# A two-layer SSM and SwiGLU kernel: five small layer-norm products move from ScalarE to VectorE, and a new order of work takes the place of the old

## The chip, the cores and the metric

The kernel runs on one core of a Trainium2 chip. A core has five engines that work through their own queues: TensorE (matrix products; PE in the profile, its weight loads PEld), VectorE (DVE), ScalarE (ACT), GpSimd (POOL) and SyncE (SP, which here only issues DMA transfers). The metric is the device time of one execution in microseconds. The kernel before took 341.52 us, the median of three runs (341.47 to 341.84).

## What is computed

Four layers follow one another on a sequence of 2048 tokens with 512 features in bfloat16, two of kind A and two of kind B, each added to its input after a layer norm without weights:

```
x = A_q
x = x + A(layernorm(x))      # A(q): kv = shift_conv(k) * v;  y = long_conv(kv, ssm_k) + kv * ssm_D;  return q * y
x = x + B(layernorm(x))      # B(x): (silu(x @ w_gate) * (x @ w_up)) @ w_down,  512 -> 1792 -> 512
x = x + A(layernorm(x))
x = x + B(layernorm(x))
layernorm(x) = (x - mean(x)) / sqrt(var(x) + 1e-5)
```

The convolution y depends on k, v and ssm_k alone, so it is made once and both A layers use it.

## The kernel before

**Tiling.** The sequence is cut into four blocks c = 0 to 3 of 512 tokens, and a block into two halves h of 256 tokens (two rows of 128 tokens by 512 features in a tile `xc`). A unit of work is (layer, c, h). For each unit there are, in this order: the layer norm of A (`apply_norm`, L958), the product with the convolution `Yk` and the sum into `xc`, the layer norm of B (both in `prologue`, L967), a transpose of its result `z` to `zT` by DMA, and the feed-forward part `ffn` (L1124). There TensorE writes gate and up products to four PSUM buffers `pf`, ScalarE empties them (`sg` by Silu and `hr` or `ht` by a copy, L1111, L1112, L1171, L1175), VectorE multiplies the two (L1115, L1118, L1178), and TensorE multiplies by `w_down` into `pd` (L1198). Some groups turn `hr` back by a DMA transpose (L1120) into `sg`. The convolution (`conv`, L1441) goes through spectra: small Fourier products on TensorE, then long products and sums on VectorE (`product`, L719: `t<-X,G` at L744, `t<-t,t` and `Z<-t,t` at L748).

**A layer norm.** Each half needs mean and variance of its two rows. `ln_stats` (L895) takes them on VectorE, into a tile `mv`. `ln_stats_act` (L906) takes them on ScalarE with two passes over each row (`jk`), and ends with `nm` (minus the mean) and `ve` (variance plus eps). Either way `power` (L888, L891) then has GpSimd raise the 128x2 values to the power -0.5: this is the tile `rstd`. There are 32 such power steps in a run, 12 from `ve` and 20 from `mv`. The rows are then normalised (`normalise`, L944) by VectorE, which reads `rstd` (L952), or by ScalarE, which reads `rstd` and a shift `nmr`, minus the mean times `rstd` (L947). `shift_of` (L932) makes `nmr`: for statistics of VectorE as one operation of VectorE (L936), for statistics of ScalarE as two operations of ScalarE, one for each row (L940). The second kind occurs in five units: the norms of A in (0,0,0), (0,0,1), (0,3,0), (1,0,0) and (1,1,1), so L940 runs ten times.

**The order.** Every operation is entered by `add` with an engine, a cost and what it reads and writes. A list `ORDER` of 1721 numbers, written out in the file, gives each operation its place in one sequence, and each engine works through its own operations in that sequence. Nothing is sorted at run time: an engine whose next operation is not ready waits, with all that is queued behind it. `walk` (L230) goes through the sequence when the kernel is built, with the entered costs. What it works out is used for two things: which buffer of a ring each tile gets, and where the 33 filler products at the start stand (`issue`, L299). It does not change the order.

**GpSimd in the walk.** A VectorE operation that touches neither PSUM nor the norm's small statistics tiles is marked `two` (L187). `walk` lets a power step (`o.late` 1 from `mv`, 4 from `ve`) wait for one such VectorE operation that is under way when it begins, then ends it (`settle`, L237).

**In numbers of the sequence.** The power step of unit (1,0,0) stands at place 362, right behind its `ve` at 353. The two `nmr` on ScalarE stand at 368 and 371, with ScalarE's emptying of `pf` before, between and behind them (366, 367, 374, 382).

Of the kernel before, what the change touches and what calls it, by code (L numbers as in the profile page):

```python
# [32 lines left out]
TINY = 0.2  # L33
# [116 lines left out]
class Plan:  # L150
# [79 lines left out]
    def walk(self, seq, loads):  # L230
# [12 lines left out]
        for o in seq:  # L243
            if pend is not None and (o.eng == "POOL" or pend in o.preds):
                settle(0.0)
                pend = None
# [83 lines left out]
def kernel(  # L330
# [14 lines left out]
    nc = tc.nc  # L345
# [1171 lines left out]
```

## Time and profile before

| what | value |
|---|---|
| median of three runs | 341.52 us |
| the profiled execution, its own time | 341.52 us |
| its span, first to last instruction | 339.7 us |
| around the span | 1.8 us |
| TensorE busy | 333.5 us, 98% |
| VectorE busy | 299.7 us, 88% |
| ScalarE busy | 264.2 us, 78% |
| GpSimd busy | 35.5 us, 10% |
| granted TensorE clock | 1.00 |
| power steps from `ve` | 12, shortest 688, median 927, longest 5031 ns |
| power steps from `mv` | 20, shortest 685, median 770, longest 1031 ns |
| `nmr` on ScalarE (L940) | 10, median 294 ns |
| `nmr` on VectorE (L936) | 7, median 154 ns |

Lines of the profile name a place in the code (L891), an engine, an operation, the tile written and, behind an arrow, the tiles read. "x10" is a count. In a list of waits, the first name is the instruction that waited and the second what it waited for, and then come the total in us, the number of waits and the longest. In a timeline, the first number is the start and the second the length, and a bracket tells how long the engine had been idle and what released it.

### The profile page before, as it was taken

The page shows a single profiled execution, that of the slowest core. Times are in us where ns is not written, and L with a number is a line of the kernel's source. Part 1 is how long each engine was busy: PE and PEld are TensorE (multiplying, and loading weights), DVE is VectorE, ACT ScalarE, POOL GpSimd, SP SyncE. Part 2 cuts the span into 40 slices and gives each one's busy share as a digit, 9 for nine tenths or more (in the row PEclk, how much of TensorE's full clock was granted, in tenths as well). Part 3 has the DMA queues.
Part 4 walks back from the last instruction along what each step waited for, and adds up shares of the span by engine and source line. Part 5 has one row for each costly group of instructions (what it writes and reads, how often), then busy time and mean ns, then how long its engine had stood idle before and what let it go on. Part 6 is the DMA issues. An engine that isn't in the chain of part 4 may idle for free.

```text
span 339.7 us, 5935 instructions
## 1 busy us (share of the span) xinstructions
PE 333.5 (98%) x2172; PEld 204.9 (60%) x2172; DVE 299.7 (88%) x507; ACT 264.2 (78%) x544; POOL 35.5 (10%) x48
## 2 busy tenths in 40 slices
PE   9999999799999999999999999999999999999996
PEld 7766864544545564745445464654546587858884
DVE  7899999799788999999999999999998887966465
ACT  7999999698996675979899985989675547465373
POOL 4000112303010100102110100002001000100000
PEclk9999999999999999999999999999999999999999
DMA  7999602251417445382324244420504430123011
GB/s 271 339 294 367 122 8 56 51 127 39 94 31 96 93 108 125 62 147 59 62 43 83 46 92 127 93 48 3 105 17 94 65 78 11 39 48 77 2 34 62
DMA packets 77992, 31.59 MB, mean 93 GB/s; under 512 B 69765, under 2 KB 75786, under 8 KB 77962
## 3 DMA queue, kind: packets, MB, share of 16 engines
q1 hardware_dynamic: 77808, 31.13, 39.5%
q8 instruction: 17, 0.28, 0.3%
q14 instruction: 13, 0.11, 0.1%
q10 hardware_dynamic: 154, 0.07, 0.1%
HBM read 12.33 MB, written 2.10 MB: 42 GB/s over the span
## 4 chain that ended last, share of the span: by engine, by line
PE 89%; DVE 5%; ACT 3%; POOL 1%; DMA 1%; issue 1%
PE pf L402 54%; PE pd L1198 20%; PE ps L1073 7%; PE ps L402 6%; POOL rstd L891 1%; DVE t L734 1%; PE wm L1483 1%; DVE Z L738 1%; DMA sg<-hr 1%; DVE m L875 1%; PE pt L569 0%; DVE bst L900 0%; ACT jk L924 0%; DVE G L537 0%; ACT sg L1111 0%
## 5 line engine op out<-in xcount | busy, mean ns | idle before, releaser
L402 PEld LDWEIGHTS <-zT 128*128 128x128 bf16 x528 | 51.5, 98 | 60.6 <-DMA zT<-z 1.0
L402 PE MATMUL pf<-wu_sb,zT 128*128 128x512 bf16 x264 | 65.3, 379 | 0.0
L402 PE MATMUL pf<-wg_sb,zT 128*128 128x512 bf16 x264 | 65.2, 379 | 0.0
L1198 PE MATMUL pd<-wd_sb,sg 128*128 128x512 bf16 x200 | 49.3, 379 | 0.1
L402 PE MATMUL pf<-zT,wu_sb 128*128 128x256 bf16 x368 | 46.1, 272 | 1.8 <-ACT sg L1111 1.6
L1111 ACT ACTIVATE sg<-pf 128x512 bf16<-128x512 f32 x66 | 39.2, 611 | 10.0 <-PE pf L402 8.3
L402 PE MATMUL pf<-zT,wg_sb 128*128 128x256 bf16 x368 | 46.1, 273 | 0.0
L1112 ACT CAST hr<-pf 128x512 bf16<-128x512 f32 x66 | 38.1, 598 | 8.6 <-PE pf L402 7.8
L402 PEld LDWEIGHTS <-wu_sb 128*128 128x128 bf16 x368 | 36.0, 98 | 9.8 <-issue 2.6
L744 DVE TENSOR_TENSOR t<-X,G 128x4096 bf16<-128x4096 bf16 x18 | 41.1, 2285 | 0.0
L402 PEld LDWEIGHTS <-wg_sb 128*128 128x128 bf16 x368 | 36.0, 98 | 7.3
L1175 ACT CAST ht<-pf 128x512 bf16<-128x512 f32 x46 | 26.8, 598 | 12.1 <-PE pf L402 10.1
L1198 PEld LDWEIGHTS <-sg 128*128 128x128 bf16 x200 | 19.4, 98 | 22.3 <-DMA sg<-hr 1.0
L891 POOL TENSOR_TENSOR rstd<-mv,nhalf 128x2 f32<-128x2 f32 x20 | 16.7, 835 | 150.5 <-DVE mv L901 139.5
L1171 ACT ACTIVATE sg<-pf 128x512 bf16<-128x512 f32 x46 | 27.1, 614 | 6.5 <-PE pf L402 5.7
L1198 PE MATMUL pd<-wd_sb,ht 128*128 128x512 bf16 (+1 forms) x126 | 29.9, 369 | 0.0
L891 POOL TENSOR_TENSOR rstd<-ve,nhalf 128x2 f32<-128x2 f32 x12 | 15.2, 1268 | 121.5 <-ACT ve L928 121.5
L900 DVE BATCH_NORM_STATS2 bst<-xc 128x6 f32<-128x512 bf16 x40 | 26.5, 683 | 0.6
L1178 DVE TENSOR_TENSOR ht<-ht,sg 128x512 bf16<-128x512 bf16 (+1 forms) x31 | 16.6, 546 | 9.4 <-ACT ht L1175 7.5
L1118 DVE TENSOR_TENSOR hr<-hr,sg 128x1024 bf16<-128x1024 bf16 x27 | 18.5, 685 | 5.3 <-ACT sg L1111 3.0
L511 ACT ACTIVATE X<-ps 128x512 bf16<-128x512 f32 x32 | 19.1, 614 | 1.5 <-PE ps L402 0.9
L1198 PEld LDWEIGHTS <-ht 128*128 128x128 bf16 x126 | 12.3, 98 | 12.2 <-ACT z L947 0.2
(143 smaller groups left out, 528.3 us busy)
## 6 DMA issues: line engine op xcount, KB each, us to landing
hn<-in_A_ssm_k_dram SPq DMA_DIRECT2D x4, 512.0 KB, 6.0
vt<-in_A_v_dram SPq DMA_DIRECT2D x4, 512.0 KB, 8.8
xc<-in_A_q_dram SPq DMA_DIRECT2D x4, 512.0 KB, 5.4
out_dram<-xc SPq DMA_DIRECT2D x15, 128.0 KB, 1.8
wg_sb<-in_B_w_gate_dram SPq DMA_DIRECT2D x1, 1792.0 KB
wu_sb<-in_B_w_up_dram SPq DMA_DIRECT2D x1, 1792.0 KB, 7.9
wd_sb<-in_B_w_down_dram SPq DMA_DIRECT2D x1, 1280.0 KB
sg<-hr SPq DMA_TRANSPOSE x66, 2.4
```

Source lines behind the costliest of these rows:

```text
L402: nc.tensor.matmul(o, lhsT=lhsT, rhs=rhs, start=(n == 0), stop=(n == len(terms) - 1))
L511: add("ACT", act(D), lambda: nc.scalar.activation(out=view(), in_=ps.t[:], func=ACT.Copy, scale=scale), r=[ps], w=[(buf, keys)], conv=conv)
L744: dve(8 * D, lambda t=t, part=part: nc.vector.tensor_mul(out=t.t[:], in0=x.t[:, :, part:part + 1, :].to_broadcast((P, R, 2, D)), in1=g.t[: ...
L891: add("POOL", cost, lambda: nc.gpsimd.tensor_tensor(out=rstd.t[:], in0=var(), in1=nhalf.t[:].to_broadcast((P, n)), op=ALU.pow), r=reads + ...
L900: add("DVE", 0.6, lambda st=st, i=i: nc.vector.bn_stats(out=st.t[:, 0:6], in_=xs[c].t[:, i, :]), r=[(xs[c], (i,))], w=[st])
L1073: nc.tensor.matmul(bank.t[:, half_ * C:(half_ + 1) * C], lhsT=lhsT(i), rhs=rhs(i), start=(first and i == 0 and half_ == 0), stop=(last and ...
L1111: add("ACT", act(D), lambda ps=ps, dst=dst, o=o, which=which: nc.scalar.activation(out=rows(dst, o), in_=ps.t[:], func=ACT.Silu) if which ...
L1112: out=rows(dst, o), in_=ps.t[:], func=ACT.Silu) if which == "g" else nc.scalar.copy(out=rows(dst, o), in_=ps.t[:]),
L1118: dve(n * W, lambda: nc.vector.tensor_mul(out=hr.t[:], in0=hr.t[:], in1=sg.t[:]), [sg], [hr], due=(unit, k / pairs, 0.0, "h"))
L1171: add("ACT", act(D), lambda ps=ps, o=o, sg=sg: nc.scalar.activation(out=sg.t[:, o:o + 2, :], in_=ps.t[:], func=ACT.Silu), r=[ps], w=[(sg, ...
L1175: add("ACT", act(D), lambda ps=ps, o=o, ht=ht: nc.scalar.copy(out=ht.t[:, o:o + 2, :], in_=ps.t[:]), r=[ps], w=[(ht, (o // 2,))], due=(uni ...
L1198: nc.tensor.matmul((pds[o] if not cs.start else pds[HP]).t[:, cs], lhsT=ht.tiles(q, o), rhs=wt["d"].t[:, ft, cs], start=(ft == std0 and no ...
```

## The change

`shift_of` no longer has ScalarE make `nmr` from its own statistics. One VectorE operation multiplies the 128x2 tiles `nm` and `rstd`:

```diff
         else:
-            for o in range(n):
-                add("ACT", TINY, lambda o=o: nc.scalar.mul(out=nmr.t[:, o:o + 1], in_=mean.t[:, o:o + 1], mul=rstd.t[:, o:o + 1]),
-                    r=[mean, rstd], w=[(nmr, (o,))], due=due)
+            add("DVE", 0.08, lambda: nc.vector.tensor_mul(out=nmr.t[:], in0=mean.t[:], in1=rstd.t[:]), r=[mean, rstd], w=[nmr], due=due)
         return nmr
```

So ten operations of ScalarE go and five of VectorE come, and `ORDER` has 1716 numbers. All of them are new: the list is another permutation.

```diff
 ORDER = [
-    6, 53, 44, 124, 2, 7, 4, 12, 24, 1, 3, 0, 17, 18, 30, 10, 8, 11, 9, 15, 27, 21, 19, 16, 20, 29, 32, 34, 40, 31, 56, 78, 22, 46, 14, 36, 23, 49,
...
+    7, 79, 141, 188, 2, 3, 1, 15, 23, 4, 12, 0, 5, 13, 68, 9, 10, 6, 8, 11, 28, 19, 14, 24, 20, 25, 32, 33, 38, 69, 144, 146, 18, 46, 17, 45, 22, 43,
...
 ]
```

`walk` treats power steps in another way: a step stays pending while VectorE runs `two` operations back to back, and is ended only when VectorE pauses (for steps from `ve`; those from `mv` still wait for one operation).

```diff
-        pend, vec, landed = None, [], 0.0
+        pend, held, vec, landed = None, 0.0, [], 0.0
...
-                settle(0.0)
+                settle(held if pend.late == 1 or pend in o.preds else max(held, pend.start) + 1.2)
...
-                if pend is not None and (o.start >= pend.start + 0.08 or (o.two and o.end > pend.start)):
-                    settle(0.0 if o.start >= pend.start + 0.08 else o.end)
-                    pend = None
+                if pend is not None:
+                    if held > 0.0 and o.two and o.start <= held + 0.03:
+                        held = o.end
+                    elif held > 0.0 or o.start >= pend.start + 0.08:
+                        settle(held)
+                        pend = None
+                    elif o.two and o.end > pend.start:
+                        held = o.end
+                        if pend.late == 1:
+                            settle(held)
+                            pend = None
...
```

Read off the new list: each engine has the same operations as before but for the ten and the five. The queue of SyncE begins with the same twelve transfers, and its last six are the same too; in between, transfers for the later convolution blocks change places (the load of `kTb` for block 3 is the 63rd transfer instead of the 73rd, that of `vt` for block 3 the 83rd instead of the 71st, and the four `hs` of block 3 come two to twelve transfers later). TensorE has 26.7 us of work by its entered costs ahead of the first feed-forward product, against 26.5 us in the old list.

In unit (1,0,0) the power step is at place 350, behind `ve` at 349. VectorE has four operations between it and the new `nmr` at 364: two `X<-m` of L638 and one of L649 (352, 355, 356) and one `hr<-hr,sg` (360). ScalarE has four operations between `ve` and the first `n<-xc,nmr,rstd` at 369: `hr` (359), `jk` (361), `ht` (362) and `sg` (367). In unit (0,0,0), in the start of the run, twelve VectorE operations of the first convolution stand between the power step (134) and its `nmr` (165). In (0,3,0) none stands between them, in (0,0,1) and in (1,1,1) one of 128x2048.

More of the change, by code (lines that the diff above doesn't have):

```diff
@@ L262, in walk @@
                 vec.append(o)
-                if pend is not None and (o.start >= pend.start + 0.08 or (o.two and o.end > pend.start)):
-                    settle(0.0 if o.start >= pend.start + 0.08 else o.end)
-                    pend = None
+                if pend is not None:
[9 more added lines that the diff above has]
+                            pend = None
             if o.late in (1, 4):
-                pend, n = o, len(vec) - 1
+                pend, held, n = o, 0.0, len(vec) - 1
                 while n >= 0 and vec[n].start >= o.start + 0.08:
@@ L270, in walk @@
                 if n >= 0 and vec[n].two and vec[n].end > o.start:
-                    settle(vec[n].end)
-                    pend = None
+                    held = vec[n].end
+                    k = n + 1
+                    while o.late == 4 and k < len(vec) and vec[k].two and vec[k].start <= held + 0.03:
+                        held = vec[k].end
+                        k += 1
+                    if o.late == 1 or k < len(vec):
+                        settle(held)
+                        pend = None
                 elif n < len(vec) - 1:
@@ L295, in walk @@
         if pend is not None:
-            settle(0.0)
+            settle(held)
         return place, {o: (o.start, o.end) for o in self.ops}
```

126 rows, old and new, of the table ORDER are left out of this document.

## The prediction

> **What bounds the kernel now.** I read the page's busy times first, then the list of TensorE's waits, then busy times by stage, then the timeline of the one stage in which TensorE waits.
>
> ```profile
> PE 333.5 (98%) x2172; PEld 204.9 (60%) x2172; DVE 299.7 (88%) x507; ACT 264.2 (78%) x544; POOL 35.5 (10%) x48
> ```
>
> ```profile
> PE pf L402 <- ACT sg L1111: 1.6, 1, 1.6
> PE wm L1483 <- PEq L1501: 0.8, 1, 0.8
> PE ptz L1010 <- ACT ks L606: 0.5, 1, 0.5
> PE pf L402 <- ACT sg L1171: 0.2, 1, 0.2
> ```
>
> TensorE bounds it. The span is 339.7 us, PE is busy 333.5, and the 6.2 left are 0.8 ahead of the first product, 0.5 at 31 us, 1.8 in one place (1.6 and 0.2, both in the 56 to 76 stage below) and 3.0 behind the last product. The change leaves TensorE's products as they are, so only waits can go or come.
>
> ```profile
> 32.00:56.00 24.00, 23.90 (x167) 16.13 (x166) 23.83 (x33) 23.89 (x55) 2.04 (x2) 1.00 0.41 89
> 56.00:76.00 20.00, 18.20 (x107) 10.27 (x106) 17.40 (x20) 17.18 (x37) 5.80 (x2) 1.00 0.35 77
> 76.00:140.00 64.00, 64.00 (x342) 33.20 (x340) 58.43 (x89) 50.26 (x101) 5.98 (x7) 1.00 0.42 82
> 180.00:220.00 40.00, 40.00 (x239) 23.18 (x237) 39.48 (x42) 34.29 (x73) 2.08 (x2) 1.00 0.40 87
> ```
>
> The columns are the length and the busy time of PE, PEld, DVE, ACT and POOL. Outside 56 to 76, PE is full; but VectorE is nearly full as well (39.48 of 40 from 180 to 220), so it has little to give.
>
> ```profile
> 56.98 2.28 DVE L744 TENSOR_TENSOR t<-X,G 128x4096 bf16<-128x4096 bf16 x1
> ...
> 57.21 0.30 ACT L928 ACTIVATE ve<-sm,eps 128x2 f32<-128x2 f32 x1
> ...
> 57.59 5.03 POOL L891 TENSOR_TENSOR rstd<-ve,nhalf 128x2 f32<-128x2 f32 x1 [10.93 <-ACT ve L928]
> ...
> 59.18 0.69 DVE L1118 TENSOR_TENSOR hr<-hr,sg 128x1024 bf16<-128x1024 bf16 x1
> ...
> 59.78 2.29 DVE L744 TENSOR_TENSOR t<-X,G 128x4096 bf16<-128x4096 bf16 x1
> ...
> 62.65 0.29 ACT L940 ACTIVATE nmr<-nm,rstd 128x1 f32<-128x1 f32 x1 [2.72 <-POOL rstd L891]
> ...
> 64.49 0.69 DVE L1118 TENSOR_TENSOR hr<-hr,sg 128x1024 bf16<-128x1024 bf16 x1 [2.42 <-ACT sg L1111]
> 64.51 1.03 PE L402 MATMUL pf<-zT,wu_sb 128*128 128x256 bf16 x8 [1.56 <-ACT sg L1111]
> ```
>
> This is unit (1,0,0). GpSimd's power step takes 5.03 us where the median of its kind takes 0.93. It ends at 62.62, 0.55 after VectorE has ended three two-input operations that follow one another without a gap. ScalarE waits 2.72 us in front of `nmr`, with the emptying of `pf` behind it; so all four `pf` buffers fill and PE stops. In start-to-start times of PE's products the whole costs 1.73 (62.57 to 64.51, less 0.21 for one product), then 0.32, then 0.25 at 67.2, where PEld waits 0.57 for `sg<-hr`, late by VectorE's 2.42: **2.3 us**.
>
> [...]
>
> **The change, part by part.**
>
> *ScalarE's ten `nmr` go.* 10 x 0.29 = 2.9 us of ScalarE, besides its 2.72 wait. The one stage in which ScalarE is full is 32 to 56 (23.89 of 24); there PE is full too (23.90), so what ScalarE saves is worth at most 0.1 to PE. Counted 0.
>
> *VectorE's five products come.* The trace has no such TENSOR_TENSOR of 128x2. From below, nothing is shorter than the 0.06 of a tiny memset; from above, a 128x256 product takes 0.28. The nearest row is L936, same size and engine, 0.154: 5 x 0.154 = 0.8 us of VectorE. Each now waits for `rstd` in VectorE's queue, with long products behind it.
>
> ```profile
> L891 POOL TENSOR_TENSOR rstd<-mv,nhalf x20: 685/770/1031, 29.9 to 309.8; 128x2 f32<-128x2 f32 x20
> L891 POOL TENSOR_TENSOR rstd<-ve,nhalf x12: 688/927/5031, 16.4 to 240.4; 128x2 f32<-128x2 f32 x12
> L936 DVE SCALAR_TENSOR_TENSOR nmr<-mv,rstd x7: 151/154/161, 48.2 to 303.7; 128x2 f32<-128x2 f32 x7
> ```
>
> The wait is also what ends a hold: VectorE must pause in front of `nmr`, so a step is held at most for the operations ordered between. In (1,0,0) those are four of 128x1024, 0.60 apart: 2.4 us. Then 0.7 for the step, 0.15 for `nmr` and two hand-overs of 0.2 (VectorE's longest waits for rstd are 0.9 us, where a step takes 0.69): 3.65 us behind `ve`. ScalarE has hr 0.60, jk 0.87 with its read-out, ht 0.60 and sg 0.61 there, 2.7. So its wait falls from 2.72 to 0.95 at most. Before, 2.72 of ScalarE cost PE 2.3, so 0.4 was covered; 0.95 then costs **0.5**, and 0 if VectorE pauses earlier. I take 0.5, since the timeline above shows four such operations follow one another without a pause.
>
> *The start.* From 13.8 to 30.6 us the chain that ended last runs along VectorE with hardly a gap, and PE's filling work ends at 31 (the 0.5 above). In (0,0,0) the power step was read by ScalarE and cost VectorE nothing (1.08 us at 16.40). Now VectorE must wait for it. Bounds: 0, if a wait for ScalarE's `X` lets the step in earlier, and 1.1 (0.9, the longest wait of VectorE for rstd, and 0.15). VectorE's waits for rstd are 2.7, 0.3 and 0.2 us in six waits, 0.53 each: I take **0.5**.
>
> *The new order.* By the lists, VectorE reads `rstd` with no operation of its own in between in 11 places instead of 5, and in 7 instead of 3 between 76 and 258 us. At 0.4 to 0.9 us each the latter are 2.8 to 6.3 us instead of the 1.2 below.
>
> ```profile
> DVE ht L1178 <- ACT ht L1175: 2.4, 3, 1.2
> ...
> DVE z L952 <- POOL rstd L891: 0.9, 1, 0.9
> ...
> DVE nmr L936 <- POOL rstd L891: 0.3, 1, 0.3
> ```
>
> In that stretch all of VectorE's waits are 7.1 us, of which 5.9 are not for rstd. What hides the added waits is that VectorE, being later, waits less for others (ht 2.4 the largest). I count 0 and keep the case that it fails as a rival. SyncE's queue moves only loads and transposes of the later convolution blocks; PE waits nowhere for those. The end has the same last six transfers, and PE the same last products: 3.0 stays.
>
> **Sum:** 341.5 - 2.3 + 0.5 + 0.5 = **340.2 us**. It is made against the profiled execution: 341.52, span 339.7, and 1.8 around it that I keep. The median of the runs shown is 341.52 too.
>
> **The rivals.**
>
> 1. *All of it hides.* No wait in the start, none in (1,0,0), perhaps less of the 0.5 at 31 us: 341.5 - 2.3 = 339.2, or 338.7 without those 0.5. For it: past 68 us, PE's starts show only two gaps until the end (0.18 at 152 and 0.10 at 244), so an order can run with almost no waits. Against: VectorE has no slack in the start. 0.15.
>
> 2. *VectorE becomes the bound* between 76 and 258 (slower). Seven direct waits at 0.9 are 6.3, less 1.2: 5.1 more, and two new `nmr` in the stretch, 0.3: 5.4. The 2.4 us that VectorE waited at 64.49 come back with the stall. If the 5.9 of other waits give nothing, VectorE is 3.0 behind, and PE waits for it before 258; ScalarE's 0.5 in (1,0,0) is then part of that: 340.2 - 0.5 + 3.0 = 342.7. The time passes that of before once the other waits give back less than 1.2 (339.7 + 1.8 = 341.5). For it: 39.48 of 40. Against: waits of a late engine shrink. 0.22.
>
> 3. *The stall only changes place.* Another power step, or a DMA that PE then waits for, costs what the old one did: 2.3: 339.2 + 2.3 = 341.5. Where no hold was behind the old wait, it comes back with the same 2.3, and the time is the same. 0.12.
>
> 4. *The start is held in full and a second place stalls:* 339.2 + 1.1 + 2.3 + 0.5 = 343.1. All 1716 places are new, and the trace of before shows none of their joints. 0.13.
>
> The forecast (339.5 to 340.8) has 0.38.
>
> **How the numbers follow.** A measurement of this kernel can tell about 0.2%, 0.7 us, from no change. Faster by more (under 340.8): 0.38 and 0.15, 0.53. Within: 0.12. Slower (over 342.2): 0.22 and 0.13, 0.35. For 8 in 10 the range goes from rival 1 without the 0.5 at 31 us and the 0.2 at 152, 338.5, to just past rival 4, 343.4. Since both signs hold much, the forecast's own range is 339.5 to 340.8.
>
> **What would show it.** Right: no wait of ScalarE for rstd or nmr over 1 us; the longest step from `ve` under 3.3 us; PE over 19.4 busy in 56 to 76; L940 gone, five `nmr` products of about 0.15; VectorE's waits for rstd in total 4 to 10 us instead of 3.2, and its other waits smaller. Wrong: PE waits for VectorE's products (`Z`, `m`, `X`) after 76 us (rival 2), another step over 3 us with PE idle behind it (3), or PE idle over 1.5 us near 31 us (4).

## The result, and the profile after

The kernel after takes 339.74 us (median of six runs, 339.51 to 339.99) where the kernel before takes 341.60 beside it (341.47 to 341.86). The ratio is 0.9944, interval 0.9931 to 0.9957: 0.56% faster, 1.9 us. The profiled execution took 339.51, its span 337.7, and again 1.8 lies around the span.

The busy times of the page after, then the list of TensorE's waits (total, times, longest):

```profile
PE 330.9 (98%) x2141; PEld 204.6 (61%) x2172; DVE 299.9 (89%) x512; ACT 262.8 (78%) x534; POOL 35.4 (10%) x48
```

```profile
PE ps L416 <- DMA kTb<-in_A_k_dram: 0.8, 1, 0.8
PE wm L1495 <- PEq L1513: 0.8, 1, 0.8
PE pd L1210 <- DMA sg<-hr: 0.3, 1, 0.3
PE ps L416 <- ACT ks L620: 0.2, 1, 0.2
```

The 1.6 and 0.2 us for `sg` are gone. In their place stand a wait for the load of `kTb` at 22 us, which lies in the filling work of the start, and 0.3 for a transposed `sg` at 241 us. The page counts 2141 products where TensorE makes 2172 (the weight loads beside it count them): 31 records are missing, a gap of one product about every 10 us, and the busy times below are short by that. I therefore compare starts of products.

The busy times of the stage of 56 to 76 us, columns as in the prediction:

```profile
56.00:76.00 20.00, 19.84 (x115) 11.36 (x116) 19.82 (x25) 19.85 (x42) 2.01 (x2) 1.00 0.52 112
```

From 56 to 76 all of PE, DVE and ACT are now full. Unit (1,0,0) in the timeline after:

```profile
56.73 0.29 ACT L942 ACTIVATE ve<-sm,eps 128x2 f32<-128x2 f32 x1
56.84 0.68 DVE L663 TENSOR_TENSOR X<-m 128x1024 bf16<-128x1024 bf16 x1
...
57.10 0.97 POOL L905 TENSOR_TENSOR rstd<-ve,nhalf 128x2 f32<-128x2 f32 x1 [9.77 <-ACT ve L942]
...
57.53 0.69 DVE L1130 TENSOR_TENSOR hr<-hr,sg 128x1024 bf16<-128x1024 bf16 x1
...
58.14 0.15 DVE L953 TENSOR_TENSOR nmr<-nm,rstd 128x2 f32<-128x2 f32 x1
```

The power step takes 0.97 us, not 5.03, and ends at 58.07. VectorE's `nmr` at 58.14 follows `hr` without a wait, so `nmr` did not end this hold. The step came in at 57.52, 0.55 before its end, where `X<-m` ended and `hr` had not begun: `hr` needs a cast of ScalarE's that ended at 57.50. That pause of VectorE's is 0.005 us long, and whether it was needed isn't shown: the step began 0.42 us ahead of the end of `X<-m`, and in twelve other places of the two profiles a step that began 0.42 to 0.51 us ahead of such an end got in there although VectorE did not pause (more on these in the last section).

In the start, unit (0,0,0), it went the other way:

```profile
20.15 4.36 POOL L905 TENSOR_TENSOR rstd<-ve,nhalf 128x2 f32<-128x2 f32 x1 [13.43 <-ACT ve L942]
```

```profile
20.11 0.68 DVE L889 TENSOR_TENSOR m<-Z 128x1024 bf16<-128x1024 bf16 x1
20.71 1.88 DVE L748 TENSOR_TENSOR t<-X,G 128x1024 bf16<-128x1024 bf16 x3
22.52 1.42 DVE L752 TENSOR_TENSOR Z<-t,t 128x512 bf16<-128x512 bf16 x4
24.55 0.16 DVE L953 TENSOR_TENSOR nmr<-nm,rstd 128x2 f32<-128x2 f32 x1 [0.61 <-POOL rstd L905]
```

Each group starts some 0.08 us before the one ahead of it has ended, up to 23.94; then VectorE waits 0.61 us for `rstd`, and the step is over 0.57 after that pause began. Here VectorE's wait for its product did end the hold.

**Where the time went.** I take each start of a product less the sum of the products ahead of it, as in the prediction's start-to-start reckoning: what is added to it is TensorE's loss. Before, it was 6.34 us at the first `pf`, then 2.29 in 64 to 68 us, 0.17 at 152 and 0.09 at 244. After, it is 6.40 at the first `pf`, nothing in 56 to 76, and 0.49 at 241. So the change is + 0.06 - 2.29 + 0.23 = -2.00, and the two profiled executions differ by 341.52 - 339.51 = 2.01.

### The profile page after: what moved, and what is told of

Read it like the earlier page. It is cut to its first block, busy times and chain, and to the rows that moved or that the text cites. A ratio compares the mean times of both kernels' runs of the same rounds, so it can differ in the third digit from the quotient of the medians.

```text
span 337.7 us, 5898 instructions
## 1 busy us (share of the span) xinstructions
PE 330.9 (98%) x2141; PEld 204.6 (61%) x2172; DVE 299.9 (89%) x512; ACT 262.8 (78%) x534; POOL 35.4 (10%) x48
## 4 chain that ended last, share of the span: by engine, by line
PE 91%; ACT 4%; DMA 2%; issue 1%; DVE 1%; SPq 1%
PE pf L416 56%; PE pd L1210 20%; PE ps L1085 7%; PE ps L416 6%; DMA kTb<-in_A_k_dram 1%; PE wm L1495 1%; DMA sg<-hr 1%; ACT H L525 1%; SPq L1132 1%; ACT ks L620 1%; ACT n L959 0%; ACT jk L929 0%; DVE t L748 0%; ACT ev L525 0%; ACT hr L1124 0%
## 5 line engine op out<-in xcount | busy, mean ns | idle before, releaser
L416 PE MATMUL pf<-wg_sb,zT 128*128 128x512 bf16 x255 | 64.3, 379 | 0.5
L416 PE MATMUL pf<-wu_sb,zT 128*128 128x512 bf16 x260 | 64.3, 379 | 0.2
L1210 PE MATMUL pd<-wd_sb,sg 128*128 128x512 bf16 x189 | 48.1, 379 | 0.9 <-DMA sg<-hr 0.3
L914 DVE BATCH_NORM_STATS2 bst<-xc 128x6 f32<-128x512 bf16 x40 | 26.5, 683 | 0.5
L525 ACT ACTIVATE X<-ps 128x512 bf16<-128x512 f32 x32 | 18.4, 604 | 1.6 <-PE ps L416 0.9
```

What stands on the lines that cost most here:

```text
L416: nc.tensor.matmul(o, lhsT=lhsT, rhs=rhs, start=(n == 0), stop=(n == len(terms) - 1))
L525: add("ACT", act(D), lambda: nc.scalar.activation(out=view(), in_=ps.t[:], func=ACT.Copy, scale=scale), r=[ps], w=[(buf, keys)], conv=conv)
L914: add("DVE", 0.6, lambda st=st, i=i: nc.vector.bn_stats(out=st.t[:, 0:6], in_=xs[c].t[:, i, :]), r=[(xs[c], (i,))], w=[st])
L1210: nc.tensor.matmul((pds[o] if not cs.start else pds[HP]).t[:, cs], lhsT=ht.tiles(q, o), rhs=wt["d"].t[:, ft, cs], start=(ft == std0 and no ...
```

## The experiments

Three theories were to be told apart: that VectorE's wait in front of its own product ends the hold; that the new order does, by a pause in another place; and, for the hold itself, that VectorE's two-input operations shut the power step out for as long as they follow one another without a pause. Each ratio is to the kernel before as it ran beside that run, with medians from 341.22 to 341.53 us (341.60 beside the kernel after), so runs are best compared by their ratios.

### The product alone, in the old order

The old order and the old `walk`, with VectorE's five products at the places of ScalarE's first ones.

```diff
-                add("ACT", TINY, lambda o=o: nc.scalar.mul(...
+            add("DVE", 0.08, lambda: nc.vector.tensor_mul(out=nmr.t[:], in0=mean.t[:], in1=rstd.t[:]), ...
 ORDER = [ ... the old one, without five entries ]
```

> The old order and the old planner, with the five products on VectorE, each at the place of ScalarE's first product. Pause theory: in unit (1,0,0) VectorE now stops in front of the product right behind the last X<-m, at 55.9 us, and waits until the power step, ready at 57.6, is over: the step takes 0.7 instead of 5.0, ScalarE's 2.7 us wait is gone, but VectorE has lost 2.5 us ahead of hr and t, so sg comes 2 to 3 us later to TensorE. I expect 340.5 to 342.5, with a TensorE wait for the transposed sg in place of the one for pf. Rival (what counts is that ScalarE no longer stands in front of rstd): 339.2 to 339.7, the whole 2.3 gained.

Measured: 342.33 us, ratio 1.0033 (1.0015 to 1.0051), slower than before. The hold is gone, and VectorE pays for it (its timeline in the profiled execution):

```profile
59.05 0.16 DVE L944 TENSOR_TENSOR nmr<-nm,rstd 128x2 f32<-128x2 f32 x1 [2.26 <-POOL rstd L892]
```

The step is 0.69 long, but VectorE had nothing to do for 2.26 us, and `hr` behind it was late. TensorE then waited 2.0 us for `sg<-hr`, 1.5 of it at once. In a second place, at 39.4 us, VectorE waited 0.58 us in front of another of the five products and ran on without a pause; at 49 to 50 us TensorE then lost 0.75, with 0.6 of waiting for VectorE's `ht`, where it lost nothing before. What came next was not in the expectation. The stages of 2 us from 64 on (behind the length stand PE, PEld, DVE, ACT, POOL and the granted clock):

```profile
64.00:66.00 2.00, 1.44 (x14) 1.04 (x11) 2.00 (x3) 0.88 (x2) 0.00 (x0) 1.00 0.48 96
66.00:68.00 2.00, 1.04 (x4) 0.31 (x4) 1.93 (x4) 0.94 (x2) 0.00 (x0) 1.00 0.50 101
68.00:70.00 2.00, 1.34 (x3) 0.58 (x5) 2.00 (x8) 1.47 (x5) 0.77 (x1) 0.59 0.42 85
70.00:72.00 2.00, 2.00 (x6) 0.70 (x5) 2.00 (x2) 2.00 (x4) 0.00 (x0) 0.56 0.25 50
```

After 4 us in which PE was busy 2.5, the granted clock fell to 0.59 and 0.56, and eight products stood 0.40 to 0.43 us apart instead of 0.22, which cost 1.6 us. This execution took 343.76, 1.4 above the kernel's median. Of the eleven executions, four show a mean clock of 0.994 or 0.995 and took 343.2 to 345.0; the other seven, at 0.999 or 1.0, took 341.6 to 342.9, and the median of these seven, 342.0, is 0.5 us above the kernel before instead of 0.8. PE had worked for most of the 4 us ahead of the fall, and its longest single wait there was 1.51; what brought the clock down isn't shown.

So the product by itself is no gain. The hold it ends is paid for by VectorE.

### The new order with (1,0,0)'s products back on ScalarE

```diff
+NMR_ACT = {(1, 0, 0)}
...
+        elif on_act:
+            ... ScalarE's two products, for (1, 0, 0) alone
```

> The kernel after, with the two products of unit (1,0,0) alone back on ScalarE, at the place of VectorE's product in the new order. Pause theory: the step of this unit came in at 57.5 us at a pause of VectorE in front of hr, ahead of the product, so nothing changes: 339.5 to 340.0, step about 1.0 us. Rival (VectorE's wait for rstd is what ends the hold, and with it gone VectorE runs on through X<-m and t<-X,G until 61.2): step about 4.7 us, ScalarE waits 3 us, TensorE some 2.6: 342 to 342.6.

Measured: 339.91 us, ratio 0.9949 (0.9937 to 0.9961), as the kernel after. The step is short again without a VectorE `nmr`, and ScalarE's does not wait:

```profile
57.77 0.96 POOL L906 TENSOR_TENSOR rstd<-ve,nhalf 128x2 f32<-128x2 f32 x1 [9.77 <-ACT ve L943]
```

In (1,0,0) it is the order that lets the step in. By which of its properties, the pause ahead of `hr` (0.01 us here) or the moment at which the step begins, stays open.

### A pause alone

The kernel before, with one copy of `rstd` on VectorE behind `hr`, so that VectorE must wait for the step there.

```diff
+        if (layer, c, h) == (1, 0, 0):
+            add("DVE", 0.08, lambda: nc.vector.tensor_copy(out=pause.t[:], in_=st[1].t[:]), r=[st[1]], w=[pause])
```

> The kernel before, with one VectorE operation more: a 128x2 copy of rstd of unit (1,0,0) into a tile that nothing reads, behind hr (place 373), so that VectorE pauses there. ScalarE still makes all ten products. Pause theory: the step ends 0.55 us behind hr, at 60.4 instead of 62.6, ScalarE waits 0.5 instead of 2.7, of which TensorE feels 0 to 0.3: 339.2 to 339.8. Rival (what counts is that ScalarE does not make the products, or the new order as a whole): 341.3 to 341.9, no change.

Measured: 339.88 us, ratio 0.9959 (0.9945 to 0.9973), 0.1 above the expectation's upper end. ScalarE's wait falls from 2.72 to 0.5, and one operation of 0.17 us in the old order does nearly all that the change does:

```profile
62.05 0.17 DVE L964 COPY pause<-rstd 128x2 f32<-128x2 f32 x1 [0.58 <-POOL rstd L891]
```

### The new walk alone

The old order, ScalarE's products, and the new `walk`, which then changes which buffer of a ring a tile gets. One thing more differs, against what is expected below: in three units ScalarE's second product moves up to right behind its first, past two of ScalarE's operations in (0,0,0), one in (1,0,0) and three at 248 us.

```diff
-                    settle(0.0 if o.start >= pend.start + 0.08 else o.end)
+                    if held > 0.0 and o.two and o.start <= held + 0.03:
...
```

> The old order and ScalarE's ten products with the new planner, which then only gives tiles other buffers. Pause theory: the same instructions in the same queues, the step of unit (1,0,0) again about 5 us, no change: 341.2 to 341.9. Rival (the gain came from other buffers): 339.5 to 340.5.

Measured: 341.21 us, ratio 0.9992 (0.9983 to 1.0000); the step takes 5.01 us and TensorE waits 1.4 and 0.2 for `sg`, much as before. The places of the buffers do next to nothing; whether the 0.3 us below the kernel before are theirs, the moved products' or chance isn't settled.

### The chain meant to be longer

```diff
 VectorE in (1,0,0): ... hr   t2
+                               t1<-t1,t2   t1<-t1,t2
```

> The kernel before, with VectorE's two t1<-t1,t2 operations of unit (1,0,0) (1.22 us each) moved ahead to right behind t2, so that VectorE's chain of two-input operations there runs about 2.3 us longer without a pause. Theory (the power step gets in only where VectorE's chain ends): the step takes about 7.3 us instead of 5.0, ScalarE waits about 5.0 us in front of nmr instead of 2.7, TensorE about 4.6 us in all instead of 2.3, and the time is 343.5 to 344 us, more if the granted clock falls behind that wait. Rival (the step's length is its own or hangs on something other than VectorE's chain): the step stays at 5.0 us and the time at 341.5.

Measured: 341.30 us, ratio 0.9999 (0.9990 to 1.0008), and the step 5.02 us. The theory missed as I had put it, and the timeline tells why:

```profile
59.87 2.29 DVE L744 TENSOR_TENSOR t<-X,G 128x4096 bf16<-128x4096 bf16 x1
62.19 2.36 DVE L748 TENSOR_TENSOR t<-t,t 128x2048 bf16<-128x2048 bf16 x2
```

The moved operation reads what the one ahead of it writes, so it starts 0.03 us after that has ended (62.16) and not 0.08 before. The step came in there and ended at 62.70. A pause of 0.03 us, which the timeline does not mark as idle, was enough here. So this run did not lengthen the chain, and a longer one was not tried.

### A write, two inputs, one input

The same place behind `hr` in the kernel before, with three short operations that wait for nothing. First a memset:

```diff
+        if (layer, c, h) == (1, 0, 0):
+            add("DVE", 0.2, lambda: nc.vector.memset(pause.t[:], 0.0), w=[pause])
```

> The kernel before, with a VectorE memset of a 128x256 bf16 scratch tile, which reads nothing and waits for nothing, put between hr and t2 of unit (1,0,0). Theory A (what lets the step in is a boundary with an operation that has no second input, whether or not VectorE pauses): the step gets in within 0.1 us of hr's end and ends about 0.55 us later, ScalarE waits under 0.7 us, TensorE about 0.3 instead of 2.3, and the time is 339.5 us. Theory B (only an idle VectorE lets it in, and the memset overlaps its neighbours): the step lasts 5.0 us or a little more, and the time is 341.5 to 342.

Measured: 339.33 us, ratio 0.9943 (0.9929 to 0.9956).

```profile
58.99 0.69 DVE L1121 TENSOR_TENSOR hr<-hr,sg 128x1024 bf16<-128x1024 bf16 x1
59.65 0.17 DVE L964 MEMSET pause<- 128x128 uint32 x1
59.73 2.23 DVE L744 TENSOR_TENSOR t<-X,G 128x4096 bf16<-128x4096 bf16 x1
```

```profile
57.40 2.82 POOL L891 TENSOR_TENSOR rstd<-ve,nhalf 128x2 f32<-128x2 f32 x1 [10.94 <-ACT ve L928]
```

VectorE does not pause: the memset begins 0.03 before `hr` ends, and the next product before the memset ends. The step still came in there (57.40 + 2.82 - 0.55 = 59.67), and no time was lost at 64 us. Then an addition of two inputs, and a copy of one:

```diff
+            add("DVE", 0.2, lambda: nc.vector.tensor_add(out=pause.t[:], in0=ident.t[:], in1=ident.t[:]), r=[ident], w=[pause])
```

> The kernel before, with a VectorE addition of two settled 128x128 bf16 inputs into a scratch tile, which waits for nothing, between hr and t2 of unit (1,0,0), where the memset of the earlier experiment stood. Theory (two-input operations that overlap shut the step out; a write without inputs let it in because it has no second input): the step is held as before, to the pause behind t2, and takes 5.0 to 5.4 us, ScalarE waits 2.7 to 3.0, and the time is 341.4 to 342. Rival (any short operation, or one more boundary, lets it in): the step takes about 2.8 us and the time is 339.3.

```diff
+            add("DVE", 0.2, lambda: nc.vector.tensor_copy(out=pause.t[:], in_=ident.t[:]), r=[ident], w=[pause])
```

> The same place, with a VectorE copy of one settled 128x128 bf16 input instead. Theory A (only a second input shuts the step out): the copy lets it in as the memset did, the step takes about 2.8 us, ScalarE waits 0.5, and the time is 339.3. Theory B (any read does): the step is held to the pause behind t2, 5.0 to 5.4 us, and the time is 341.4 to 342.

Measured: 341.59 us, ratio 1.0014 (1.0002 to 1.0026) with the addition, and 339.28, ratio 0.9940 (0.9927 to 0.9954) with the copy. Operation and step with the addition:

```profile
59.70 0.22 DVE L964 TENSOR_TENSOR pause<-ident 128x128 bf16<-128x128 bf16 x1
```

```profile
57.52 5.14 POOL L891 TENSOR_TENSOR rstd<-ve,nhalf 128x2 f32<-128x2 f32 x1 [10.95 <-ACT ve L928]
```

and with the copy:

```profile
60.02 0.22 DVE L964 COPY pause<-ident 128x128 bf16<-128x128 bf16 x1
```

```profile
57.84 2.86 POOL L891 TENSOR_TENSOR rstd<-ve,nhalf 128x2 f32<-128x2 f32 x1 [10.94 <-ACT ve L928]
```

Both take 0.22 us and add one boundary; what differs is the second input (an addition instead of a copy), and the two steps differ by 2.3 us. TensorE's loss from 56 to 76 us goes with them: 2.4 us with the addition, 0.1 with the copy. So in this place it is operations with two inputs, following one another without a pause, that shut the step out. With the addition the step was shut out past three ends of operations (59.17, 59.78 and 59.92) and came in at the fourth, at 62.11. By what means a row of operations does that isn't shown.

### The new order alone

The order and the `walk` of the kernel after, and all ten products on ScalarE.

```diff
-            add("DVE", 0.08, lambda: nc.vector.tensor_mul(out=nmr.t[:], ...
+            for o in range(n):
+                add("ACT", TINY, lambda o=o: nc.scalar.mul(...
```

> The order and the buffer places of the kernel after, with all ten products on ScalarE, at the places where the kernel after has VectorE's products. Theory (a product of VectorE's ends the hold only where the order has no pause of its own, which is in unit (0,0,0) alone): ScalarE waits there in front of nmr until the step gets in, from 1.9 us (if it gets in at the pause in front of m) up to 3.8 (if it is held to the end of the chain), the start takes 0 to 3.4 us longer, and the time is between 339.8 and 343 us; (1,0,0) keeps its short step of under 1.5 us. Rival (where the products are done matters nowhere, the order does all): 339.6 to 340.0.

Measured: 344.29 us, ratio 1.0083 (1.0069 to 1.0097), the slowest of all and beyond the theory's range. ScalarE's three waits for a step:

```profile
25.02 0.48 ACT L955 ACTIVATE nmr<-nm,rstd 128x1 f32<-128x1 f32 x2 [1.96 <-POOL rstd L906]
```

```profile
41.78 0.48 ACT L955 ACTIVATE nmr<-nm,rstd 128x1 f32<-128x1 f32 x2 [0.80 <-POOL rstd L906]
42.16 1.06 ACT L1188 ACTIVATE sg<-pf 128x512 bf16<-128x512 f32 x2
```

```profile
228.96 0.48 ACT L955 ACTIVATE nmr<-nm,rstd 128x1 f32<-128x1 f32 x2 [1.35 <-POOL rstd L906]
```

The first is the held step of (0,0,0), 4.37 us long, and TensorE has lost 3.4 us more than in the kernel after by 43 us. The second, in unit (0,0,1), is no hold: the step takes 0.69. But `sg` stands behind `nmr`, and TensorE waits 1.0 us for it and loses 1.2, where the kernel after, with `sg` ahead and `nmr` on VectorE, loses nothing. The third I had not seen: at 229 us the statistics come late and the step takes 1.18, of which only a part is a hold; with `nmr` in ScalarE's queue its copies of `X` and `dn` behind are late, and TensorE loses another 1.4 us there. (1,0,0) keeps its short step, 0.81.

To see whether the hold makes the first part, the memset went into the chain of (0,0,0), right behind the first `m`:

```diff
+        if (layer, c, h) == (0, 0, 0):
+            add("DVE", 0.2, lambda: nc.vector.memset(pause.t[:], 0.0), w=[pause])
```

> The kernel with the changed order and all ten products on ScalarE, with the same memset at the same place as in the run beside this one. Theory (of the 2.9 us that this order loses with the products on ScalarE, the part at the start comes from the held step alone): ScalarE's wait of 2.0 us in front of the first nmr is gone, TensorE's loss between 24 and 43 us falls by 2 to 3.4 us, that near 230 to 246 us (1.4 us more than in the kernel after) stays, and the time is 340.9 to 342.2. Rival (the start is late for another reason, such as ScalarE's own work): 344.0 to 344.4, unchanged.

Measured: 341.94 us, ratio 1.0022 (1.0014 to 1.0031). ScalarE's wait at the start is gone, and TensorE's loss up to the same product, at 43 and now at 40 us, falls from 9.77 to 7.20, by 2.6 us. The 1.35 at 226 us stays. The other 0.8 of the 3.4 is not the hold's: ScalarE still waits 0.80 us in (0,0,1), where no step is held, and TensorE still loses 1.2 there; with that, a little less is lost ahead of it than in the kernel after.

### The kernel after, with the same memset

> The kernel after, with a VectorE memset of a 128x256 bf16 scratch tile right behind the first m of unit (0,0,0), in the chain that holds the step there for 4.4 us. Theory (the write lets the step in; nothing on the path that sets the end waited for it): the step takes under 1.5 us, VectorE's wait of 0.6 us in front of nmr is gone, and the time stays at 339.6 to 339.9. Rival (that wait costs TensorE what it costs VectorE): 339.1 to 339.3.

Measured: 339.00 us, ratio 0.9937 (0.9924 to 0.9951), the lowest time of all; but its interval overlaps that of the kernel after (0.9931 to 0.9957), so that it is faster isn't shown. As a time it missed the theory's range and lies even below the rival's. The kernel before took 341.22 beside it, so by the ratio 0.9944 the kernel after would stand at 339.3 there; the time can't tell the two apart, and the trace has to.

```profile
20.09 1.22 POOL L905 TENSOR_TENSOR rstd<-ve,nhalf 128x2 f32<-128x2 f32 x1 [13.37 <-ACT ve L942]
```

The step of (0,0,0) falls from 4.36 to 1.22 and VectorE's wait goes, yet between 22.8 and 33 us TensorE loses 0.71 in both kernels. What differs between the two profiled executions lies elsewhere: 0.47 ahead of that, where the wait for `kTb` is 0.4 instead of 0.8, and 0.30 lost at 241 instead of 0.49. The theory holds for the wait: nothing on the path that sets the end stood behind it.

### The wait at 241 us

In the kernel after, SyncE's fourth transpose of `sg` for unit (1,2,0) is queued behind one of `zT`. I changed the two about.

```diff
 SyncE: sg sg sg
-       zT sg zT
+       sg zT zT
```

> The kernel after, with SyncE's fourth transpose of sg of unit (1,2,0) issued ahead of the transpose of zT that stands in front of it in the queue. Theory (TensorE's wait of 0.3 us at 241 us, worth 0.49 us with what follows, comes from that place in the queue alone): the wait is gone and the time is 339.2 to 339.5 us. Rival (the zT that comes later, or the next transfer, is late in its turn): 339.7 us, unchanged.

Measured: 340.74 us, ratio 0.9979 (0.9970 to 0.9988): a miss. It is 1.0 us above the kernel after, and the intervals do not overlap. The wait moved to the transfer that had been put back:

```profile
PE pf L416 <- DMA zT<-z: 0.9, 1, 0.9
```

TensorE lost 1.10 us there, and at 241 still 0.31. From 234.2 to 243.2 us SyncE issues transposes one behind the other, so the order among these only chose which was late.

## Why the prediction was right, and where not

**The bound, and the 2.3 us that go: right.** The loss of 2.29 in 64 to 68 us went in full, and nothing took its place there. That this is the hold's price, the pause, the memset and the copy show: in the old order each brings the step to 2.8 or 2.9 us and the time to 339.3 to 339.9.

**What ends the hold in (1,0,0): wrong in the mechanism.** The step that failed is "VectorE must pause in front of `nmr`, so a step is held at most for the operations ordered between". It read places in the order as times. When the step began, at 57.10, two of the four operations had ended and the third was 0.26 us old; the step got in at its end, ahead of `hr`, and with ScalarE's products it did just so (339.91). The lines given there for "four such operations" show three two-input operations in a row, one of them of 128x1024. The quoted sentence holds in (0,0,0), where the hold ran through eight operations to VectorE's wait. Its term, +0.5 for ScalarE's 0.95, measured 0: no wait of ScalarE for `rstd`, none for that `nmr`.

**The start: too dear.** Predicted +0.5, measured +0.06. VectorE did wait, 0.61, inside the bounds of 0 and 1.1; the step that failed is the sum's assumption that what VectorE loses there TensorE loses too. The kernel after with the memset shows the same loss of TensorE without that wait. The +0.06 itself is small against what the start varies by: up to 36 us TensorE loses 3.1 to 4.3 us in the four profiles with the new order and VectorE's product in (0,0,0), and 3.2 to 5.1 in the seven with the old order and ScalarE's. The sign "no step of `ve` over 3.3 us" was wrong for the same reason: the step of 4.36 lies in the unit for which I had worked out VectorE's wait from its waits elsewhere, and not from the chain of operations ahead of its `nmr`.

**The new order costs 0 in 76 to 258: nearly.** VectorE's direct waits for `rstd` there are 2.9 us (2.8 to 6.3 were reckoned), so rival 2 lacked its 5.4. Its other waits fell only from 5.9 to 5.5: the others gave back 0.4 of the 1.7 us that were added, not all of it as I had argued. No loss of TensorE's is traced to the remaining 1.3, so VectorE seems to have had that much to spare; where, no run shows. In the whole run the waits for `rstd` are 5.9 instead of 3.2:

```profile
DVE z L964 <- POOL rstd L905: 2.8, 5, 0.8
...
DVE n L964 <- POOL rstd L905: 1.5, 2, 0.9
```

TensorE's balance there is 0.49 at 241 less the 0.26 at 152 and 244: +0.23, not reckoned.

**ScalarE's 2.9 us and VectorE's five products: right.** The products take 0.14 to 0.16 each, the 0.154 of the nearest row:

```profile
L953 DVE TENSOR_TENSOR nmr<-nm,rstd x5: 143/153/161, 24.6 to 225.9; 128x2 f32<-128x2 f32 x5
```

**The sum.** 340.2 - 0.44 (start) - 0.5 ((1,0,0)) + 0.23 (241 us) = 339.5, the profiled execution's 339.51. So two terms of half a microsecond each were near nothing, for reasons that the prediction did not have; that the forecast was only 0.5 too high is in part luck, since they were small beside the 2.3.

**The rivals.** The time lies between the forecast and rival 1 (339.2), that all hides. Rival 2 was decided by the direct waits. Rival 3's case that no hold was behind the old wait is excluded by the addition and the copy: with the addition the step took 5.14 us, past three ends of operations, and with the copy 2.86, and the two times differ by 2.3 us. Of rival 4, the start was held (the step of 4.36), but TensorE did not pay for it, and no second place stalled for more than 0.49. The parts, taken singly, were worse than before (342.33 and 344.29); together they gain 1.9, because in the new order the step of (1,0,0) gets in early, and VectorE's products keep the steps of (0,0,0), of (0,0,1) and of 229 us off ScalarE's queue. For (0,0,0) the memset tests that; for (0,0,1) and 229 us it rests on comparing the two runs that have ScalarE's products there with those that have VectorE's.

## What to carry to other kernels

When a tiny GpSimd step takes several times its median (here 5.03 us against 0.93), look at the VectorE operations beside it for a row of two-input operations that overlap (here three, by 0.08 us); one short VectorE operation with one input or none, put into that row, can be worth as much as a new order (here ratios of 0.9940 and 0.9943 against 0.9944). A wait is best given to the engine that has nothing urgent queued behind it at that place, and that is read place by place: in the new order the same product on ScalarE cost nothing in (1,0,0), some 2.6 us in (0,0,0) as long as the step there was held, and 1.2 in (0,0,1) with a step that was not held. In the one run that moved a transfer ahead in a busy DMA queue, another became late and cost more (1.10 us of TensorE's, against 0.49).

## What the runs showed of the hardware that was not expected

- The power step of (1,0,0) ended about 0.55 us after the VectorE operation that it waited for: 62.07 to 62.62 before, 57.52 to 58.07 after, 62.16 to 62.70 in the run meant to lengthen the chain.
- On VectorE, operations that read the result of the one ahead started 0.03 us after its end (154.98 and 155.02 before, 62.16 and 62.19 in the run meant to lengthen the chain), and independent ones in the chains that held a step about 0.08 before it (59.26 and 59.18 before, 20.79 and 20.71 after). The timeline marks neither as idle. The overlaps from 59.18 before and from 20.71 after let no step in; the 0.03 us at 62.16 did.
- Not every such overlap held a step. In twelve places of the two profiles, steps that began 0.42 to 0.51 us ahead of the end of a two-input operation got in there, although the next one, with two inputs as well, had already started (0.97 to 1.08 us long). Where that end came 1.68 us after the step had begun (57.59 before) or 0.64 (20.15 after), the step did not get in; at 191.46 after, where it came at 0.68, it did (1.23 long). So the distance alone doesn't decide, and no run was made for it.
- TensorE's granted clock fell to 0.56 behind a stretch of 4 us in which it was busy 2.5, in the one execution of the product alone in the old order whose trace shows it; three more of that kernel have nearly as low a mean clock (0.995 against 0.994).
